# One order of summing and turning the values' product, a new hand-written order of attention, more zero matmuls in the bias stage

## The chip, the core and the metric

The kernel runs on one core of a Trainium2 chip. The metric is device time in microseconds (us). Before the change three runs took 933.37 to 933.82 us, median 933.52 us.

## What is computed

Four batches of 576 positions go through attention with 8 heads of 64, then an MLP with layer norm (512 to 2048 to 512), then a gated MLP that mixes positions. Everything is float32. The part around the change, cut:

```python
scores = scale * q @ k.T                       # per batch and head, 576 x 576
x = log1p(|i - j|) / log1p(max(i, 1))
scores += relu(x[..., None] * w1 + b1) @ w2    # one bias matrix per head
attn = exp(scores - max); attn /= attn.sum(-1) + 1e-9
out = attn @ v                                 # back to rows of 512
x = out + relu(layernorm(out) @ w_ch1) @ w_ch2
...
```

## The kernel before, in words

Products that need float32 accuracy are done in pieces: a value is split into a part rounded to the fast matmul type (hi) and a rest (lo), and hi x hi, lo x hi and hi x lo are added in PSUM.

**Stages.** (1) The bias stage builds the bias of all heads: VectorE (line 335) and ScalarE (line 333) make relu pieces, TensorE sums them over the hidden units (line 347), VectorE or ScalarE scales them (lines 354, 356), and DMAs write them to DRAM and read them back in the layout of the scores. Matmuls of zeros (`busy`, line 293) are put in at the start (`WARM` = 8) and ahead of the sums of the steps in `FILL` (9 of the 36 steps, one each). (2) Attention runs over 16 units: a unit is a pair of heads (hp) of one batch (b), in the order hp outer, b inner. (3) The first MLP, (4) the gated MLP.

**One attention unit** has nine score tiles n = 0 to 8 of 128 query rows (tile 4 holds the last 64 rows of both heads). For a tile, S is the scores' matmul (line 705, four of 288 columns, eight for n = 4), add is the bias add with the row minimum on VectorE (line 711), exp is ScalarE's exponential with the row sum (line 725), T turns the 128x512 weights in four transposes (line 731), hi is ScalarE's rounded copy out of PSUM and lo is VectorE's rest (lines 118, 121). The last 64 keys go another way: RT turns them (lines 739, 741), RThi and RTlo split them, and RTd (lines 769, 771) is a DMA that moves the rest to the other half of the partitions; RTx splits straight into place instead of RTlo and RTd. PV multiplies with the values (line 813), nine matmuls for each head h and half x of the columns; the rt one is the ninth.

**The end of a unit before the change.** The values are stored as hi and lo side by side, so PV gives 128 rows: 64 of the main part and 64 of the lo part, still turned (head dimension on partitions). Pev (line 816, ScalarE) copies 128x288 to `Psb`. O (line 819) turns a 128x128 block of one head, four per head, eight per unit. Oev (line 824, ScalarE) copies the four blocks to `Ob`. fo (line 830, GpSimd) adds the two parts, once per head. fx (line 842, GpSimd) multiplies by the reciprocal row sum, once per head, and a DMA stores 512 rows to DRAM (line 845). The last 64 rows go by oc, Or (line 853), xr (lines 862, 863) and stores at line 867. ra and rb make the reciprocals.

**What sets the order.** Each engine takes its instructions in the order in which the program emits them, and so does the SP queue, from which nearly all DMAs are issued: a DMA that waits holds up those behind it. Lists of words give that order: `FIRST` for unit 0, `SEQ` for every later unit ("0 T 3" is this unit's tile 3, "-1" the unit before, "1" the unit after), `END` for the tail of unit 15 with the first MLP tiles (H). `slot n` marks a place where side work is issued: at slot 0 `place_q` (line 237) puts the next unit's queries in place with four DMAs, at slot 1 the stores of line 867, at slot 5 the loads of a later unit's q and k. kh and vh split the next unit's keys and values on GpSimd, sq splits queries. C and cp are steps of converting the MLP's weights (line 161 to 178, five VectorE steps per piece, two steps in each of units 2 to 11). The rows of attention's output of batch 0 are read back for the MLP (four DMAs, line 626) at slot 8 of unit 13, those of batch 1 at slot 8 of unit 15, and layer norm is spread behind them.

The score tiles alternate between two PSUM buffers (`SB`) and the transposes between two (`PA`), so S of a tile waits for the add two tiles earlier, and T for the lo two tiles earlier.

Of the kernel before, what the change touches and what calls it, by code (L numbers as in the profile page):

```python
# [43 lines left out]
    PV 0 1 8 9, hi 8, slot 7, +S 4, lo 7, +exp 1, slot 8, Pev 0 1
# [57 lines left out]
def block_kernel(  # L102
# [484 lines left out]
    def open_first():  # L587
# [32 lines left out]
        for b in range(2):  # L620
            x = M["x", b] = []

            def loads(b=b, x=x):
                for t in range(4):
                    x.append(M["stage"].tile([128, DM], F32, name="t"))
                    sp.dma_start(out=x[t], in_=xs[b][128 * t:128 * t + 128])

            M["loads", 12 + 2 * b] = loads
        for q, j in enumerate(LN_AT):
            for (b, t) in j:  # L630
                v, j = 13 + (q + 1) // 2, (q + 1) % 2
                if v == 14:
                    conv_at.setdefault((v, 2), []).append(lambda b=b, t=t: ln_stats(b, M["x", b][t], M["x", b][t], act if b else pool))
                    continue
                then = conv_at.setdefault((v, j + 1), []).append
                conv_at.setdefault((v, j), []).append(lambda b=b, t=t, f=then: ln_stats(b, M["x", b][t], M["x", b][t], act if b else pool, f))
        for t, p in enumerate(AP_AT):
            when(*p, lambda t=t: ln_apply(0, t))
# [825 lines left out]
```

## Time and profile before

| | |
|---|---|
| median of three runs | 933.52 us |
| profiled execution, its own time | 936.71 us |
| its span from first to last instruction | 934.9 us |
| TensorE matmul busy | 914.6 us, 98% of the span |
| VectorE / ScalarE / GpSimd busy | 716.4 / 494.7 / 419.0 us |
| chain that ended last | TensorE 86%, VectorE 6%, DMA 3% |

The profile is of one execution, which has a time of its own. Busy shares are averages over stages with different limits, so they are read by stage. A matmul's duration holds the time in the pipeline; what a matmul adds to a run of them is the distance from one start to the next.

### The profile page before, as it was taken

Reading aid. Unit: us, or ns where it says so; the run is one execution under the profiler, and the core shown is the slowest. Engines: PE = TensorE matmul, PEld = TensorE weight load, DVE = VectorE, ACT = ScalarE, POOL = GpSimd, SP = SyncE. Lnnn points to the kernel's source line nnn. Section 1 sums busy time; section 2 is a strip of 40 time slices with the busy share of each in tenths; the row PEclk is TensorE's granted clock in tenths of the full one; section 3 lists DMA queues with packets and bytes.
Section 4 is the critical chain, followed back from the end, with each engine's and each line's share of the span. In section 5 each row is a group of like instructions: output and inputs, shape, how many; then the busy total and the mean of one; then the engine's idle time right before and its main releaser. Section 6 shows DMA issues by size and latency. Waiting matters only on the chain.

```text
span 934.9 us, 15977 instructions
## 1 busy us (share of the span) xinstructions
PE 914.6 (98%) x5617; PEld 798.7 (85%) x5617; DVE 716.4 (77%) x1390; ACT 494.7 (53%) x1092; POOL 419.0 (45%) x547
## 2 busy tenths in 40 slices
PE   7899999999999999999999999999999999999998
PEld 2279999999998888888888888888888998989996
DVE  7999999999888777877689897989665656455452
ACT  8989999999997653222131322222132635253340
POOL 0058888888897543322233343333200534243241
PEclk9999999999999999999999999999999999999999
DMA  6888767767762641121212323342313000001001
GB/s 222 283 265 276 238 189 243 218 210 216 231 197 63 214 163 46 56 89 34 89 56 89 126 87 123 101 123 89 102 68 127 1 1 34 12 1 57 1 35 67
DMA packets 64623, 113.18 MB, mean 121 GB/s; under 512 B 13216, under 2 KB 27680, under 8 KB 64288
## 3 DMA queue, kind: packets, MB, share of 16 engines
q1 hardware_dynamic: 64240, 111.74, 37.9%
q8 instruction: 44, 0.72, 0.3%
q10 hardware_dynamic: 304, 0.43, 0.1%
q14 instruction: 35, 0.29, 0.1%
HBM read 70.33 MB, written 28.38 MB: 106 GB/s over the span
## 4 chain that ended last, share of the span: by engine, by line
PE 86%; DVE 6%; DMA 3%; POOL 2%; ACT 2%; issue 1%; SPq 0%; POOLq 0%; DVEq 0%; ACTq 0%
PE psh L125 21%; PE psy L125 21%; PE psa L125 11%; PE s L705 6%; PE psa L1308 6%; PE PB L813 6%; PE psa L1290 5%; PE pt L731 5%; DVE m L335 4%; PE pt L486 1%; PE OB L819 1%; DMA q<-q 1%; DMA rt<-tl 1%; PE s L741 1%; PE pt L347 1%
## 5 line engine op out<-in xcount | busy, mean ns | idle before, releaser
L125 PE MATMUL psh<-blk,w1h 128*128 128x512 f32 (+1 forms) x640 | 151.2, 368 | 0.0
L654 ACT ACTIVATE hh<-psh 128x512 fp32r<-128x512 f32 (+1 forms) x80 | 44.1, 554 | 198.6 <-PE psh L125 198.5
L177 POOL TENSOR_TENSOR cvl<-cvl,cvt 128x512 f32<-128x512 f32 x44 | 56.9, 1293 | 205.4 <-DVE cvt L174 185.9
L125 PEld LDWEIGHTS psh<-blk,w1h 128*128 128x128 f32 x640 | 113.4, 189 | 20.5
L725 ACT ACTIVATE a<-ct,sm 128x576 f32<-128x576 f32 x144 | 112.1, 781 | 2.6 <-DVE sm L711 2.6
L711 DVE CUSTOM_DVE_ANT_0 ct<-s,bias 128x576 f32<-128x576 f32 x144 | 106.3, 747 | 5.4 <-PE s L705 3.5
L1111 DVE TENSOR_TENSOR x_sb<-psy,x_sb 128x512 f32<-128x512 f32 x144 | 97.3, 683 | 9.5 <-PE psy L125 9.0
L655 DVE SCALAR_TENSOR_TENSOR hl<-psh,hh 128x512 fp32r<-128x512 f32 (+1 forms) x80 | 50.5, 633 | 57.2 <-ACT hh L654 57.2
L125 PE MATMUL psy<-w2h,hh 128*128 128x512 f32 x288 | 90.1, 394 | 0.0
L125 PE MATMUL psy<-w2l,hh 128*128 128x512 f32 x288 | 88.9, 390 | 0.0
L125 PE MATMUL psy<-w2h,hl 128*128 128x512 f32 x288 | 88.8, 389 | 0.0
L731 PE MATMUL pt<-ident,a 128*128 128x128 f32 x576 | 84.4, 274 | 0.4 <-DVE at0l L121 0.4
L125 PE MATMUL psh<-blk,w1l 128*128 128x512 f32 (+1 forms) x320 | 79.0, 368 | 0.0
L705 PE MATMUL s<-kh,q 128*128 128x288 f32 x320 | 75.3, 325 | 3.2 <-DMA q<-q 2.1
L731 PEld LDWEIGHTS pt<-ident,a 128*128 128x128 f32 x576 | 68.6, 142 | 1.1 <-DVE at0l L121 0.7
L705 PE MATMUL s<-kl,q 128*128 128x288 f32 x320 | 65.7, 295 | 0.0
L125 PEld LDWEIGHTS psh<-blk,w1l 128*128 128x128 f32 x320 | 56.8, 189 | 10.0
L125 PEld LDWEIGHTS psy<-w2h,hl 128*128 128x128 f32 x288 | 54.1, 188 | 11.5
L125 PEld LDWEIGHTS psy<-w2l,hh 128*128 128x128 f32 x288 | 54.0, 188 | 11.5
L178 POOL TENSOR_TENSOR cvw<-cvl,cvw 128x512 f32<-128x512 f32 x44 | 59.9, 1362 | 3.4
L125 PEld LDWEIGHTS psy<-w2h,hh 128*128 128x128 f32 x288 | 52.6, 188 | 9.6
L121 DVE TENSOR_TENSOR at1l<-pt,at1h 128x512 fp32r<-128x512 f32 (+1 forms) x80 | 50.3, 630 | 9.3 <-ACT at1h L118 9.2
(185 smaller groups left out, 2126.7 us busy)
## 6 DMA issues: line engine op xcount, KB each, us to landing
r<-in_moe_w_ch_dram SPq DMA_DIRECT2D x32, 512.0 KB, 4.6
k<-in_k_dram SPq DMA_DIRECT2D x16, 640.0 KB, 4.4
q<-q SPq DMA_DIRECT2D x64, 144.0 KB, 3.4
scr<-o SPq DMA_DIRECT2D x24, 295.5 KB, 3.4
v<-in_v_dram SPq DMA_DIRECT2D x16, 320.0 KB, 5.1
q<-in_q_dram SPq DMA_DIRECT2D x16, 288.0 KB, 3.1
wc<-cvw SPq DMA_DIRECT2D x16, 256.0 KB, 2.5
x_sb<-xs SPq DMA_DIRECT2D x4, 1024.0 KB, 7.1
```

What stands on the lines that cost most here:

```text
L121: (eng or dve).tensor_tensor(out=o, in0=i, in1=hi.bitcast(F32), op=ALU.subtract)
L125: pe.matmul(ps, lhsT=w, rhs=x, start=start and j == 0, stop=stop and j == len(terms) - 1)
L177: pool.tensor_tensor(out=T["l"], in0=T["l"], in1=T["t"].bitcast(F32), op=ALU.mult)
L178: pool.tensor_tensor(out=T["w"], in0=T["l"], in1=T["w"], op=ALU.add)
L655: dve.scalar_tensor_tensor(out=hl[:, f, :n], in0=ps[:, :n], scalar=0.0, in1=hh[:, f, :n].bitcast(F32), op0=ALU.max, op1=ALU.subtract)
L705: pe.matmul(s[:, x, :288], lhsT=w, rhs=m[:, 288 * x:288 * x + 288], start=j == 0, stop=j == len(prs) - 1)
L711: dve.tensor_tensor_reduce(out=ct, in0=s[:, :, :288], in1=bias[UNITS[u][0]][:, n].rearrange("p (a b) -> p a b", a=2), scale=-0.125, scalar ...
L725: act.activation(weights(n), ct.rearrange("p a b -> p (a b)"), AF.Exp, scale=-1.0, bias=mt, accum_out=SU[u % 2][:, n:n + 1])
L731: pe.transpose(PA[k % 2][:, j], e[:, 128 * j:128 * j + 128], ident)
L813: pe.matmul(d, lhsT=w, rhs=m, start=q == 0, stop=q == len(terms) - 1)
L1111: dve.tensor_tensor(out=x_sb[:, t], in0=ps, in1=x_sb[:, t], op=ALU.add)
L1308: pe.matmul(ps[:, z, :288], lhsT=v, rhs=w[:, 288 * z:288 * z + 288], start=(q == 0), stop=(q == len(terms) - 1))
```

## The change

Units 1 to 14 no longer turn both parts of both heads. `Pd` moves the half of the 128 rows that has to change partitions by a DMA (64x512, one per head), `Ps` adds it to the other half on GpSimd (64x512, one per head), and the two heads' sums lie on top of each other in `whole`. Four transposes `Q` turn it, and fx multiplies by the reciprocals straight out of PSUM on VectorE. Unit 0 and unit 15 keep O, Oev and fo. `SEQ` and `END` are new, `FIRST` covers units 0 and 1 and `END` units 14 and 15 (SEQ now runs for u = 2 to 13). The reads of batch 0 and batch 1 (LD) and the layer norm steps (LN, LS, LP, FT, F) are words of `END`. `WARM` is 12, and `FILL` gives 21 zero matmuls over 14 steps. Bias loads of hp 0 are placed at other words.

```diff
-FILL = (0, 4, 8, 12, 16, 20, 24, 28, 32)
+FILL = {0: 1, 4: 1, 6: 1, 8: 6, 10: 1, 11: 1, 12: 1, 14: 3, 15: 1, 16: 1, 20: 1, 24: 1, 28: 1, 32: 1}
-WARM = 8
+WARM = 12
-            if y in FILL:
-                busy(1)
+            busy(FILL.get(y, 0))
...
+        moved, whole = (Ob[:, z].rearrange("p a b -> p (a b)") for z in range(2))
+        def emit_Pd(u, h):
+            sp.dma_start(out=moved[half(1 - h)].rearrange("p (x c) -> p x c", x=2), in_=ends(Psb[half(h), h]))
+        def emit_Ps(u, h):
+            o, i, j = (t[half(1 - h)] for t in (whole, Psb[:, h], moved))
+            pool.tensor_tensor(out=o.rearrange("p (x c) -> p x c", x=2), in0=ends(i), in1=j.rearrange("p (x c) -> p x c", x=2), op=ALU.add)
+        def ends(p):
+            return bass.AP(p.tensor, p.offset, [list(p.ap[0]), [320, 2], [1, 256]])
+        def emit_Q(u, t):
+            o = (0, 256, 128, 384)[t]
+            pe.transpose(OB[:, 128 * t:128 * t + 128], whole[:, o:o + 128], ident)
...
         def emit_fx(u):
...
+            if u not in xt:
+                x = xp.tile([128, 4, 2, D], F32, name="x")
+                z = 18 + 9 * (u % 2)
+                f = sm[:, z:z + 10].rearrange("p (h a) -> p a h", h=2)[:, :4].unsqueeze(3).to_broadcast([128, 4, 2, D])
+                dve.tensor_tensor(out=x, in0=OB.rearrange("p (a h d) -> p a h d", a=4, h=2), in1=f, op=ALU.mult)
```

The new `SEQ`, whole:

```python
0 slot 0, -1 lo 8, 0 B 0, 0 add 3, 0 exp 2, 0 T 0, 0 exp 3, -1 PV 1 0 0 5, -1 PV 1 0 5 8, -1 PV 1 0 8 9, 0 hi 0, 0 slot 1, 0 add 4, -1 Pev 1 0,
0 RT 1 0, 0 S 5, 0 exp 4, 0 RT 3 0, -1 Pd 0, 0 RThi 0, 0 C 0, 0 S 6, 0 T 1, -1 PV 1 1 0 1, 0 lo 0, 0 T 2, 0 C 1, 0 hi 1, 0 add 6, -1 PV 1 1 1 8,
0 add 5, -1 PV 1 1 8 9, 0 lo 1, 0 hi 2, 0 S 7, 0 slot 2, 0 lo 2, 0 RT 4 0, 0 exp 5, -1 Pev 1 1, 0 slot 3, 0 T 3, 0 T 4, 0 RThi 2, 0 RTlo 0, 0 kh,
-1 Pd 1, 0 S 8, 0 hi 3, 0 hi 4, 0 add 7, 0 exp 6, 1 S 0, 0 RTd 0, 0 lo 3, 0 PV 0 0 0 2, 0 T 5, 0 slot 4, 0 RTlo 2, 0 lo 4, 0 exp 7, 0 RTd 2,
0 slot 5, 0 add 8, 0 PV 0 0 2 8, 0 T 6, 0 vh, -1 oc, 1 S 1, 0 hi 5, 1 add 0, 0 exp 8, 1 S 2, 0 lo 5, 0 RT 8 1, 1 add 1, 0 RT 6 1, -1 Ps 0,
0 PV 0 0 8 9, 0 hi 6, -1 Or, -1 Ps 1, 0 lo 6, 0 T 7, 0 RThi 1, -1 ra, -1 Q 3, 0 Pev 0 0, -1 Q 0, -1 rb, 0 RTlo 1, -1 Q 1, 0 RTd 1, -1 Q 2, 0 T 8,
0 B 1, 1 add 2, 0 PV 0 1 0 8, 0 cp, 0 PV 0 1 8 9, 1 S 3, 1 S 4, -1 fx, 1 exp 0, 0 hi 7, 0 sq, 0 hi 8, 0 slot 6, 0 lo 7, 0 slot 7, -1 xr, 1 exp 1,
0 Pev 0 1, 0 slot 8
```

The part of the new `END` that the prediction speaks of (unit 14, from its start to the turns of unit 13):

```python
14 slot 0, 14 add 3, 14 exp 2, 14 exp 3, 14 LD 0 0, 14 S 5, 14 T 0, 14 hi 0, 13 lo 8, 14 LD 0 1, 14 slot 1,
...
14 S 8, 13 Ps 0, 14 RT 4 0, 13 Pev 1 0, 14 lo 2, 13 PV 1 1 0 1, 14 RTlo 0, 14 exp 6, 14 LD 0 3, 14 hi 3, 13 PV 1 1 1 8, 13 PV 1 1 8 9, 14 T 4,
14 add 8, 14 slot 5, 13 Pev 1 1, 14 RThi 2, 14 lo 3, 14 LN 1, 14 hi 4, 15 S 0, 15 S 1, 14 PV 0 0 0 2, 14 exp 7, 14 RT 6 1, 14 exp 8, 14 lo 4, 14 T 5,
14 vh, 14 RTlo 2, 14 T 6, 14 RTd 0, 14 PV 0 0 2 8, 15 add 0, 15 S 2, 13 oc, 15 add 1, 14 hi 5, 13 Pd 1, 14 lo 5, 13 Ps 1, 13 Q 2, 13 Q 1, 14 RTd 2,
...
```

## Rows read from the trace of the kernel before

**Rows 1.** The page, part 1: busy time, share of the span, instructions.

```profile
PE 914.6 (98%) x5617; PEld 798.7 (85%) x5617; DVE 716.4 (77%) x1390; ACT 494.7 (53%) x1092; POOL 419.0 (45%) x547
```

**Rows 2.** Stretches: length, busy PE, PEld, DVE, ACT, POOL (instructions), clock, DMA share, GB/s.

```profile
0.00:52.39 52.39, 40.91 (x370) 12.92 (x370) 47.01 (x132) 45.58 (x101) 2.12 (x11) 1.00 0.75 254
52.39:71.02 18.63, 17.57 (x128) 15.58 (x124) 16.91 (x41) 15.81 (x41) 11.57 (x11) 1.00 0.84 270
86.55:102.87 16.32, 15.88 (x128) 15.41 (x127) 15.31 (x36) 15.46 (x41) 13.75 (x19) 1.00 0.74 221
149.47:165.00 15.53, 15.53 (x128) 15.53 (x127) 14.41 (x36) 15.02 (x40) 14.05 (x15) 1.00 0.80 251
273.71:293.92 20.21, 18.07 (x134) 17.76 (x132) 15.76 (x39) 15.95 (x43) 14.28 (x25) 0.92 0.44 112
```

**Rows 3.** TensorE by time: start, us, operation, count, idle time before with its releaser.

```profile
130.28 1.04 PE L731 MATMUL pt<-ident,a 128*128 128x128 f32 x8
...
131.69 0.69 PE L813 MATMUL PB<-at0l,v 128*64 128x288 f32 x4
132.22 0.29 PE L813 MATMUL PB<-rt,v 128*128 128x288 f32 x1
...
284.62 0.51 PE L705 MATMUL s<-kh,q 128*128 128x288 f32 x2 [2.14 <-DMA q<-q]
```

**Rows 4.** One stretch of 1 us behind that wait; columns as in rows 2.

```profile
286.00:287.00 1.00, 1.00 (x6) 1.00 (x6) 0.97 (x4) 0.13 (x1) 0.00 (x0) 0.50 0.00 0
```

**Rows 5.** SP queue by time, ahead of that wait: start, us, DMA, count.

```profile
270.70 0.38 SPq L845 DMA_DIRECT2D xs<-x  x1
...
275.58 1.76 SPq L626 DMA_DIRECT2D t<-xs  x4
277.43 2.40 SPq L237 DMA_DIRECT2D q<-q  x4
```

**Rows 6.** Groups removed, or nearest to what is added: busy us, mean ns, idle before.

```profile
L819 PE MATMUL OB<-ident,psb 128*128 128x128 f32 x128 | 24.5, 272 | 0.0
L830 POOL TENSOR_TENSOR x<-ob 128x256 f32<-128x256 f32 x30 | 22.1, 736 | 8.6 <-ACT ob L824 5.7 <-PE pt L731 2.9
L842 POOL TENSOR_TENSOR x<-x,sm 128x256 f32<-128x256 f32 x30 | 17.9, 618 | 0.0
L121 POOL TENSOR_TENSOR vre<-v,vre 64x512 fp32r<-64x512 f32 x2 | 2.6, 1291 | 0.2
L1340 DVE TENSOR_TENSOR v<-psa,x_sb 128x512 f32<-128x512 f32 x18 | 12.4, 688 | 21.2 <-PE psa L125 13.7 <-POOL blk L121 7.5
```

**Rows 7.** VectorE by time, two neighbouring instructions inside unit 4.

```profile
125.78 0.69 DVE L121 TENSOR_TENSOR at0l<-pt,at0h 128x512 fp32r<-128x512 f32 x1
126.38 0.75 DVE L711 CUSTOM_DVE_ANT_0 ct<-s,bias 128x576 f32<-128x576 f32 x1
```

**Rows 8.** Line 771: its issue on the SP queue and its landing.

```profile
L771 SPq DMA_DIRECT2D rt<-tl x14: 634/638/657, 94.1 to 301.0; - x14
DMA to landing us min/median/max: 1.9/2.5/3.7
```

**Rows 9.** GpSimd by time in unit 14: the keys' first step, the values' last.

```profile
275.37 0.73 POOL L115 TENSOR_SCALAR kh<-k 128x640 fp32r<-128x640 f32 x1
...
282.23 1.54 POOL L121 TENSOR_TENSOR v<-v,v 128x640 fp32r<-128x640 f32 x1
```

**Rows 10.** TensorE by time in the bias stage: zeros, and the sums behind two holes.

```profile
1.03 4.21 PE L293 MATMUL pt<-zero 128*128 128x512 f32 x9 [1.03 <-DVE zero L288]
6.64 2.33 PE L347 MATMUL pt<-m,W 128*32 128x320 f32 x24 [1.41 <-DVE m L335]
...
16.25 1.68 PE L347 MATMUL pt<-m,W 128*32 128x448 f32 x16 [1.63 <-DVE m L335]
```

**Rows 11.** TensorE's waits between 73 and 310 us.

```profile
PE pt L731 <- DVE at0l L121: 0.4, 1, 0.4
PE PB L813 <- DMA rt<-tl: 0.3, 1, 0.3
```

More of the change, by code (lines that the diff above doesn't have):

```diff
@@ L44 @@
[L44 removed]
+    0 S 0, 0 add 0, 0 slot 0, 0 slot 1, 0 S 1, 0 S 2, 0 add 1, 0 exp 0, 0 T 0, 0 S 5, 0 exp 1, 0 add 2, 0 RT 1 0, 0 hi 0, 0 T 1, 0 exp 2, 0 add 5, 0 C 0,
+    0 S 3, 0 S 6, 0 lo 0, 0 C 1, 0 add 3, 0 slot 2, 0 add 6, 0 T 2, 0 exp 5, 0 slot 3, 0 S 4, 0 hi 1, 0 hi 2, 0 S 7, 0 exp 3, 0 lo 2, 0 RT 3 0, 0 exp 6,
+    0 T 3, 0 lo 1, 0 add 4, 0 RThi 0, 0 RTx 0, 0 hi 3, 0 T 5, 0 S 8, 0 kh, 0 exp 4, 0 RT 6 1, 0 hi 5, 0 slot 4, 0 RT 4 0, 0 lo 3, 0 add 7, 0 T 4, 1 S 0,
@@ L45 @@
+    2 add 1, 1 Pev 0 0, 0 Oev 1, 2 S 2, 0 fo 1, 1 RTx 1, 2 exp 0, 0 fx, 1 T 7, 0 Or, 1 sq, 2 add 2, 1 B 0, 1 T 8, 1 slot 6, 1 hi 7, 1 PV 0 1 0 8,
+    1 PV 0 1 8 9, 1 hi 8, 2 exp 1, 1 slot 7, 1 lo 7, 0 xr, 1 Pev 0 1, 1 slot 8, 2 S 3, 2 S 4
 """.split(",")]
-B_AT = [(0,), (1, 2), (3,), (4, 5), (6,), (7, 8)]
-LN_AT = [(), (), ((0, 0), (0, 1)), ((0, 2), (0, 3)), ()]
-AP_AT = [(15, 0), (15, 1), (15, 4), (15, 5)]
+B_AT = [[(), (0,), (1, 2), (3, 4), (5, 6), (7, 8)], [(0,), (1, 2), (3,), (4, 5), (6,), (7, 8)]]
@@ new lines @@
+    14 LS 0, 14 PV 0 0 8 9, 14 hi 6, 14 lo 6, 13 Or, 14 LS 1, 13 Q 3, 13 Q 0, 15 LN 2, 15 exp 0, 13 fx, 15 exp 1, 14 T 8, 14 slot 6, 14 slot 7,
+    14 RT 8 1, 14 T 7, 15 S 3, 14 ra, 14 Pev 0 0, 13 xr, 14 RThi 1, 14 hi 7, 14 slot 8, 14 hi 8, 15 add 2, 15 slot 0, 15 RT 1 0, 15 LN 3, 15 LS 2,
+    14 PV 0 1 0 8, 15 LS 3, 14 PV 0 1 8 9, 15 slot 1, 15 LP 0, 15 add 3, 14 lo 7, 15 S 4, 14 RTlo 1, 15 exp 2, 14 lo 8, 15 slot 2, 15 add 4, 15 S 5,
+    15 LP 1, 14 Pev 0 1, 14 RTd 1, 15 exp 3, 15 T 0, 15 RT 3 0, 14 PV 1 0 0 5, 15 hi 0, 15 RThi 0, 15 slot 3, 14 PV 1 0 5 8, 15 lo 0, 15 add 5, 15 T 1,
@@ new lines @@
+    15 exp 4, 15 hi 1, 15 S 6, 14 PV 1 0 8 9, 15 RTlo 0, 15 T 2, 15 lo 1, 14 Pev 1 0, 15 RT 4 0, 15 exp 5, 15 S 7, 15 slot 4, 14 PV 1 1 0 1,
+    14 PV 1 1 1 8, 15 add 6, 14 PV 1 1 8 9, 15 S 8, 15 hi 2, 15 RTd 0, 14 Pd 0, 15 exp 6, 15 add 7, 15 slot 5, 15 T 3, 14 Pev 1 1, 15 RThi 2, 15 lo 2,
+    15 LP 2, 15 RTlo 2, 14 Pd 1, 14 Ps 0, 16 FT 0, 15 add 8, 15 hi 3, 15 lo 3, 16 F 0, 15 T 4, 15 RTd 2, 15 hi 4, 15 lo 4, 16 FT 1, 15 T 5, 14 Ps 1,
+    15 PV 0 0 0 2, 16 FT 2, 15 PV 0 0 2 8, 14 rb, 15 PV 0 0 8 9, 14 oc, 14 Q 2, 14 Q 3, 15 exp 7, 16 F 1, 16 F 2, 15 hi 5, 15 Pev 0 0, 15 exp 8, 14 Q 0,
@@ L525, in ln_two @@
     def ln_two(j):
-        x = M["x", 1][2 * j:2 * j + 2]
+        x = [M["x", 1][2 * j + q] for q in range(2)]
         mv, rs = (M["two"][:, 8 * j + 4 * q:8 * j + 4 * q + 4].rearrange("p (a b) -> p a b", a=2) for q in range(2))
@@ L619, in open_first @@
         xT[0] = block_pair(M["wa0"])
[L620 to L638, printed above, removed]
+        M["x", 0], M["x", 1] = {}, {}
+        xn[0] = {}
     def h_tile(ch, blk, f, a=0, b=12):
@@ L919, in emit_slot, with emit_LD, emit_LN @@
                 open_first()
-            if n == 8 and ("loads", u - 1) in M:
-                M["loads", u - 1]()
         emit = dict(
             slot=emit_slot, B=emit_B, sq=emit_sq, kh=emit_kh, vh=emit_vh, C=emit_C, cp=lambda u: emit_C(u, 2), S=emit_S, add=emit_add, exp=emit_exp, T=emit_T, hi=emit_hi, lo=emit_lo, RT=emit_RT, RThi=emit_RThi,
-            RTlo=emit_RTlo, RTd=emit_RTd, RTx=emit_RTx, PV=emit_PV, Pev=emit_Pev, O=emit_O, Oev=emit_Oev, fo=emit_fo, fx=emit_fx, Or=emit_Or, oc=emit_oc, ra=emit_ra, rb=emit_rb, xr=emit_xr,
+            RTlo=emit_RTlo, RTd=emit_RTd, RTx=emit_RTx, PV=emit_PV, Pd=emit_Pd, Ps=emit_Ps, Q=emit_Q, Pev=emit_Pev, O=emit_O, Oev=emit_Oev, fo=emit_fo, fx=emit_fx, Or=emit_Or, oc=emit_oc, ra=emit_ra, rb=emit_rb, xr=emit_xr,
         )
+        def emit_LD(u, b, t):
+            x = M["x", b][t] = M["stage"].tile([128, DM], F32, name="t")
+            sp.dma_start(out=x, in_=xs[b][128 * t:128 * t + 128])
+        def emit_LN(u, t):
+            x = M["x", 0][t]
+            stats, scale, apply = norm_parts(M["sm"], x, 1e-6, x, pool)
+            stats()
+            xn[0][t] = x, apply, scale
         def first_T(j):
```

77 lines of the change are left out of this document (38 added, 39 removed).

## The prediction

> **What bounds the kernel now.** I read the page first: TensorE is busy for 914.6 of 934.9 us [rows 1]. A busy share says nothing about single stages, so the busy time by stretch comes next [rows 2]. In the bias stage (0 to 52.39 us) VectorE is busy for 47.01 and ScalarE for 45.58 us, TensorE for 40.91: those two set the pace there. In attention it turns round. A middle unit lasts 15.53 us and TensorE is busy for all of it; ScalarE has 15.02, VectorE 14.41, GpSimd 14.05 us. Two stretches stand out: unit 2 with 16.32 us and unit 14 with 20.21 us. The MLPs come after 312 us and the change leaves their matmuls alone. So the edit pays in attention by what it takes off TensorE, if no other engine takes over, and by the stalls that the new order avoids or adds.
>
> **Fewer transposes.** A transpose's mean duration is 272 ns [rows 6], but that holds the way through the pipeline. Eight in a row took 1.04 us [rows 3], so each further one costs (1.04 - 0.27) / 7 = 0.11 us. Four matmuls of 288 columns take 132.22 - 131.69 = 0.53 us to the next start, 0.13 each [rows 3]. The list of a unit (76 matmuls, 50 transposes) then sums to 15.47 us, against 15.53 measured [rows 2], so these prices may be used. Units 1 to 14 turn four blocks in place of eight: 14 x 4 = 56 transposes fewer, 56 x 0.11 = **-6.2 us**, and a unit of about 15.05 to 15.1 us. The Trainium skill (TensorE: Matmul & The Clock Gate, Part 4: PE-mode transpose) gives about 275 ns for one in a kernel's context; as a duration the trace agrees (272 ns), as a cost eight in 1.04 us speak against it; by it the term would be -15.4 us.
>
> **The other engines.** ScalarE loses two 128x512 copies per unit, which nobody waited for long. GpSimd loses two fo (736 ns) and two fx (618 ns), 2.71 us, and gains two Ps; an add of that very shape, 64x512, took 1291 ns [rows 6], so 2.58 us: even. VectorE gains fx. Its nearest row is a 128x512 add that reads PSUM, 688 ns [rows 6]; from start to start such an operation takes 126.38 - 125.78 = 0.60 us [rows 7]. Then VectorE has 14.41 + 0.60 = 15.0 us in a unit of 15.1. ScalarE runs today at 15.02 of 15.53 without TensorE waiting for it, so this need not fail, but there is no room: I take 0.1 us in each of the ten units with conversion steps, **+1.0 us** (bounds: 0, if the order hides it; 4, if each loses 0.4).
>
> **The stall before unit 15.** TensorE waited 2.14 us for the queries of unit 15 [rows 3]. On the SP queue the store of unit 12 went out at 270.70, the four reads of the same rows had to wait for it and went at 275.58, and the queries stood behind them until 277.43 [rows 5]. In the new order slot 0 of unit 14, which issues these queries, stands ahead of LD 0 0, so this wait goes: **-2.1 us**. What is late next is the subject of the next but one part. Behind the wait the granted clock was 0.50, so 1.2 GHz [rows 4]; over the 20.21 us of unit 14 it was 0.92 [rows 2], that is 0.08 x 20.21 / 0.5 = 3.2 us at half speed, which cost 1.6 us: **-1.6 us** if no wait like it comes in its place. The rest of unit 14's excess I leave where it is.
>
> **Unit 2** is 16.32 - 15.53 = 0.8 us too long, with a wait of 0.4 us for a lo [rows 2, 11]. It lies in the old SEQ's first turns, which the new FIRST replaces: **-0.8 us** (bound 0). The opening, 18.63 us with 17.57 busy [rows 2], is replaced too; I see nothing that decides it: 0, between -1 and +1.
>
> **A new wait in unit 14.** Now TensorE needs GpSimd inside the unit: Pev, Pd, Ps, then Q. LD 0 0 still waits for unit 12's store, which now goes out some 13 us into unit 13; 275.58 - 270.70 = 4.9 us later [rows 5] is 2.8 us into unit 14. Behind it on the SP queue stand LD 0 1 (1.76 / 4 = 0.44 us to issue), two stores of slot 1 and Pd 0, each about 0.64 us, and a DMA of this kind lands 2.5 us after its issue [rows 5, 8]: Pd 0 lands at 2.8 + 0.9 + 1.2 + 2.5 = 7.4 us. On GpSimd the run from kh to the end of v took 283.77 - 275.37 = 8.4 us from 1.66 us into unit 14 [rows 9], with one fo and a small wait in it. With two Ps in place of that fo and Ps 0 held until 7.4, Ps 1 ends at about 12.4 us. TensorE's list reaches Q 2 at 10.6 us. I take a wait of 1.8: **+1.8 us**. Bounds: 0 (GpSimd starts earlier) and 3.4 (the clock falls again for 1.6).
>
> **RTd 2.** In the new SEQ RTlo 2 comes after lo 3 on VectorE, by the summed steps at 8.2 us of a unit; its DMA lands 2.5 us later, at most 3.7 [rows 8], so at 10.7; TensorE's ninth matmul of PV 0 0, which reads it, stands at 10.7. Today such a wait occurs once in the attention, 0.3 us [rows 11]. I take 0.1 us for each of the 12 turns of SEQ, **+1.2 us** (bounds 0 and 6, with 0.5 each). RTd 1 has more room than now: the store that waits for fx stands behind it instead of ahead.
>
> **Zeros.** Nine zero matmuls took 4.21 us at the start, at most 0.47 each, and the first sums then waited 1.41 us for VectorE [rows 10]. Four more end at most 0.5 us late, five more at step 8, where 1.63 us were idle, 0.7 us late. VectorE and ScalarE set this stage, and the clock is at 1.00 all through it [rows 2]: I take 0, between 0 and +1.2; their cover is the idle time of TensorE.
>
> **Sum.** -6.2 + 1.0 - 2.1 - 1.6 - 0.8 + 1.8 + 1.2 = -6.7 us. The profiled execution took 936.71 us, which would become 930.0. The median of the runs is 3.2 us lower than that execution; the same difference on 933.52 gives **926.8 us**. 0.2% is 1.9 us, about what can be told from no change: faster means below 931.7, slower above 935.4.
>
> **Rivals.** (1) *GpSimd sets attention, slower.* In a unit kh, Ps 0, v, oc and Ps 1 take some 9.9 us and stand ahead of Q on GpSimd. TensorE reaches Q 3 at 11.4 us, so kh must start by 1.5 us. It started 1.66 us into unit 14 [rows 9]; it can start from 0.5 us, when xr of the unit before is through, because sq has to wait for less. Each microsecond beyond 1.5 costs 12 us over SEQ. The forecast turns into slower from (1.9 + 6.7) / 12 = 0.7 us per unit, that is kh at 2.2 us or two Ps of 1.65 us; at 1.0 us per unit it gives 933.5 - 6.7 + 12 = 939 us. For it: GpSimd's 14.05 of 15.53 us; against: in most units no cp is due. The Trainium skill (GPSIMD Engine Reference, 1. Specifications) says that GpSimd shares its SBUF interfaces with VectorE; no row here shows a Ps-like add above 1.29 us on average. Chance 0.10. (2) *VectorE becomes the bound, no change.* It loses 0.4 us in each of the 12 units (4.8), RTd 2 costs 0.3 (3.6, in place of 2.2 for both) and unit 14's wait brings the half clock back (+1.6): 926.8 + 6.2 + 1.6 = 934.6 at worst, 931.7 to 934.6 with part of it. For it: 15.0 of 15.1 us; against: ScalarE at 97% today costs nothing. Chance 0.11. (3) *The new waits don't come.* Then -6.2 - 2.1 - 1.6 - 0.8 = -10.7, with the opening's bound -11.7: 922 to 923. Chance 0.22. (4) *Each transpose is worth its duration:* 56 x 0.272 = 15.2 in place of 6.2, 917.8 us. Eight in 1.04 us exclude it nearly. Chance 0.02. The forecast itself, 924 to 931.7, has 0.55.
>
> **How the numbers follow.** Faster is the forecast with (3) and (4), 0.79; the same 0.11; slower 0.10. The range holds the forecast and (3), and of (2) the nearer part, so 921.5 to 933.
>
> **What would show it.** Right: 16 + 56 = 72 transposes into OB; middle units of 15.05 to 15.2 us with TensorE busy throughout; no wait of S for the queries before unit 15; a wait of Q for Ps in unit 14 of 1 to 3 us and none in the units before. Wrong: Q waiting for GpSimd in every unit (1); units of 15.4 us with T or S waiting for lo or add (2); PV's rt matmul waiting for its DMA in most units; a stretch at half clock in unit 14; a bias stage longer than 52.4 us.

## The result, and the profile after

The kernel after took 940.89 us (median of 6 runs, 939.99 to 942.47), the kernel before beside it 933.58 us (933.02 to 933.82): ratio 1.0079, 95% interval 1.0066 to 1.0092. It is **slower by 7.3 us**, where 6.7 us less were forecast, and lies outside the range. From the first MLP on nothing changed: its first transposes stand at 318.69 us in the profile before and at 322.41 us in the one after, 3.7 us later, and the spans, 934.9 and 938.8 us, differ by 3.9. The bias stage is nearly as long as before (52.39 and 52.51 us). So the question lies in attention.

Page, part 1, of the kernel after (answers to [rows 1]):

```profile
PE 915.7 (98%) x5577; PEld 794.5 (85%) x5577; DVE 726.1 (77%) x1404; ACT 486.4 (52%) x1064; POOL 419.3 (45%) x519
```

TensorE's busy share is 98% as before, and would tell nothing. Busy time by stretch, kernel after, columns as in [rows 2]: the bias stage, then three middle units.

```profile
0.00:52.51 52.51, 45.62 (x386) 16.52 (x386) 46.98 (x132) 45.59 (x101) 2.24 (x11) 1.00 0.75 252
132.69:148.39 15.70, 15.65 (x124) 15.09 (x123) 15.70 (x39) 14.44 (x37) 15.08 (x15) 1.00 0.78 217
197.68:212.86 15.18, 15.18 (x124) 15.06 (x124) 14.51 (x37) 14.08 (x37) 13.31 (x16) 1.00 0.68 186
148.39:165.04 16.65, 15.38 (x124) 15.12 (x123) 15.82 (x39) 15.07 (x39) 12.26 (x13) 1.00 0.86 255
```

The reader sees three kinds of unit. In the third row TensorE works throughout and the unit is 15.18 us, as forecast; three units are like this (15.15, 15.18, 15.11). In the second, VectorE is busy for all of 15.70 us. In the fourth, TensorE is busy for 15.38 of 16.65 us; it waits for the rest. What for is in its waits from 73 to 310 us (answers to [rows 11]):

```profile
PE PB L819 <- DMA rt<-tl: 6.6, 8, 2.7
PE OB L838 <- POOL ob L831: 2.4, 3, 1.0
PE s L711 <- DVE sm L717: 0.9, 1, 0.9
```

The ninth matmul of PV waits for the rest of the last keys eight times. Before, it did so once, for 0.3 us.

The groups that the change removes and adds, kernel after (answers to [rows 6]):

```profile
L838 PE MATMUL OB<-ident,ob 128*128 128x128 f32 x56 | 8.8, 277 | 2.4 <-POOL ob L831 2.4
L841 PE MATMUL OB<-ident,psb 128*128 128x128 f32 x16 | 3.9, 272 | 0.0
L867 DVE TENSOR_TENSOR x<-OB,sm 128x512 f32<-128x512 f32 x14 | 9.6, 686 | 1.3 <-PE OB L838 1.3
```

72 transposes into OB in place of 128, and fx on VectorE at 686 ns, as its nearest row gave.

**One late unit, followed.** Kernel after, the SP queue, then TensorE, VectorE and GpSimd by time, around the wait of 1.27 us at the end of the unit 148.39 to 165.04:

```profile
157.13 1.10 SPq L896 DMA_DIRECT2D xs<-xr  x2
158.34 0.63 SPq L827 DMA_DIRECT2D ob<-psb  x1
159.01 0.59 SPq L589 DMA_DIRECT2D r<-in_moe_w_ch_dram  x1
159.70 0.62 SPq L827 DMA_DIRECT2D ob<-psb  x1
160.42 1.19 SPq L775 DMA_DIRECT2D rt<-tl  x2
161.70 0.62 SPq L777 DMA_DIRECT2D rt<-tl  x1
```

```profile
158.39 0.41 DVE L145 TENSOR_TENSOR tl<-s,rt 128x256 fp32r<-128x256 f32 x1
...
160.05 0.27 DVE L145 TENSOR_TENSOR tl<-s,rt 64x128 fp32r<-64x128 f32 x1
```

```profile
164.83 0.37 PE L819 MATMUL PB<-rt,v 128*128 128x288 f32 x1 [1.27 <-DMA rt<-tl]
```

```profile
164.30 1.27 POOL L831 TENSOR_TENSOR ob<-psb,ob 64x512 f32<-64x512 f32 x1 [2.21 <-DMA ob<-psb]
165.66 0.20 POOL L855 TENSOR_SCALAR sm<-sm 128x9 f32<-128x9 f32 x1
```

```profile
165.89 0.22 DVE L858 RECIPROCAL sm<-sm 128x9 f32<-128x9 f32 x1 [1.68 <-POOL sm L855]
166.07 0.42 DVE L145 TENSOR_TENSOR tl<-s,rt 128x256 fp32r<-128x256 f32 x1
```

RTlo 0 is done at 158.80 us and RTlo 2 at 160.32, but SP issues one DMA behind the other and comes to RTd 0 only at 160.42 and to RTd 2 at 161.70. Pd 1, issued at 159.70 right behind a load of 512 KB, lands 4.6 us later, so Ps 1 starts at 164.30. Behind Ps 1 on GpSimd stands ra, and VectorE's rb waits 1.68 us for it; behind rb stand RTlo 1 and RTd 1. So one late transfer is handed on: SP, Pd, Ps, ra, rb, RTlo 1. VectorE waited for ra 6 times, 7.7 us, in the kernel after; before, this wait is not among VectorE's.

That SP itself is late shows at RTd 2 (line 771 before, 777 after; ns, least/median/most, of the queue's wait for RTlo 2):

```profile
L771 SPq EVENT_SEMAPHORE  x14: 28/1174/6319, 91.9 to 294.6; - x14
```

```profile
L777 SPq EVENT_SEMAPHORE  x14: 17/17/17, 96.2 to 305.2; - x14
...
who waited for it (us, times):
  PE PB L819: 5.6, 5
  PEld PB L819: 0.6, 1
```

Before, RTd 2 went out ahead of RTd 0; SP was there first and waited 1.2 us (median) for VectorE. After, both Pd and the two issues of RTd 0 stand ahead of RTd 2, and its data always waited for SP, up to 2.1 us. That alone need not cost anything: at RTd 0 SP never waited in the kernel before either, and TensorE lost 0.3 us there.

**What ended the eight waits.** Late landings ended most of them. In three units (at 110.36, 159.01 and 191.63 us) a load of 512 KB of the MLP's weights is issued between Pd 0 and Pd 1. The first of them on the SP queue, TensorE's wait behind it, and that period (columns as in [rows 2]):

```profile
110.36 0.61 SPq L587 DMA_DIRECT2D r<-in_moe_w_ch_dram  x1
111.06 0.62 SPq L827 DMA_DIRECT2D ob<-psb  x1
111.78 1.19 SPq L775 DMA_DIRECT2D rt<-tl  x2
113.06 0.99 SPq L777 DMA_DIRECT2D rt<-tl  x1
```

```profile
117.33 0.37 PE L819 MATMUL PB<-rt,v 128*128 128x288 f32 x1 [2.70 <-DMA rt<-tl]
```

```profile
99.25:117.54 18.29, 15.59 (x124) 15.12 (x123) 16.04 (x39) 15.06 (x39) 12.47 (x13) 1.00 0.90 267
```

Over all units, line 777 (RTd 2) lands so long after its issue:

```profile
DMA to landing us min/median/max: 1.9/1.9/4.1
```

In the three units Pd 1, RTd 0 and RTd 2 landed 3.0 to 5.4 us after their issue, each behind the load; in the other units between 120 and 250 us the two Pd, RTd 0 and RTd 2 took 1.9 to 2.5 us. The waits in the three units are 2.70, 1.27 and 0.39 us, 4.4 of the 6.6. Had RTd 2 landed in 1.9 us there too, some 0.6 us would be left of them (an estimate from the times of its issues). Three more waits (0.21, 0.19 and 0.68 us) are for RTd 1, which landed 4.8 to 5.3 us after its issue, shortly behind the loads of k and v. In the last two (0.92 and 0.28 us) RTd 2 landed in 2.0 us, so only SP's lateness is left. In the kernel before the same weight loads are there, but RTd 2 and RTd 0 landed in 2.0 to 3.7 us, and no wait came of it.

### The profile page after: what moved, and what is told of

It reads as the page before. It is cut to its first block, busy times and chain, and to the rows that moved or that the text cites. A ratio compares the mean times of both kernels' runs of the same rounds, so it can differ in the third digit from the quotient of the medians.

```text
span 938.8 us, 15923 instructions
## 1 busy us (share of the span) xinstructions
PE 915.7 (98%) x5577; PEld 794.5 (85%) x5577; DVE 726.1 (77%) x1404; ACT 486.4 (52%) x1064; POOL 419.3 (45%) x519
## 4 chain that ended last, share of the span: by engine, by line
PE 79%; POOL 8%; DMA 5%; DVE 4%; issue 2%; ACT 1%; SPq 0%; POOLq 0%; DVEq 0%
PE psh L149 21%; PE psy L149 21%; PE psa L149 10%; PE psa L1341 6%; PE psa L1323 5%; PE s L711 4%; PE PB L819 3%; PE pt L737 3%; DMA rt<-tl 3%; DVE m L359 2%; POOL kl L145 2%; PE pt L509 1%; POOL ob L831 1%; POOL v L145 1%; PE pt L371 1%
## 5 line engine op out<-in xcount | busy, mean ns | idle before, releaser
L711 PE MATMUL s<-kh,q 128*128 128x288 f32 x320 | 72.7, 317 | 1.8 <-DVE sm L717 1.5
L711 PEld LDWEIGHTS s<-kh,q 128*128 128x128 f32 x320 | 48.7, 189 | 5.1 <-DVE sm L717 3.0
```

The source lines that it names most:

```text
L711: pe.matmul(s[:, x, :288], lhsT=w, rhs=m[:, 288 * x:288 * x + 288], start=j == 0, stop=j == len(prs) - 1)
```

## The experiments

Ratios are to the kernel before, run beside each kernel on the same chip; its medians there were 933.6 to 935.9 us, so ratios are compared, not times. The interval behind each is 95%. The waits are those of one profiled execution of each kernel.

| kernel | us | ratio | TensorE waits for rt / Q, 73 to 340 us |
|---|---|---|---|
| after | 940.89 | 1.0079 | 6.6 / 2.4 |
| q_first | 933.11 | 0.999 | none / none |
| old_order_q | 957.73 | 1.0262 | 2.2 / 9.5 |
| old_zeros | 941.03 | 1.0068 | 7.6 / 1.1 |
| rtx2 | 939.97 | 1.0054 | 4.8 / 1.3 |
| sp_more | 942.47 | 1.0094 | 9.5 / 2.8 |
| one_store | 940.46 | 1.0069 | 5.8 / 1.9 |
| sp_late | 953.91 | 1.0198 | 17.3 / 1.7 |
| kv_late, rtx2_kv_late | 963.66, 966.13 | 1.0323, 1.0348 | not read; 7.5 / 7.6 |
| pd_act | 942.0 | 1.008 | 3.4 / 3.1 |
| ra_early | 938.85 | 1.0053 | 3.8 / 3.4 |
| ra_early_rtx2 | 938.01 | 1.0041 | 3.6 / 2.9 |
| ra_early_rtx_all | 946.13 | 1.0130 | none / 1.4 |
| no_conv | 940.25 | 1.0055 | 6.3 / 2.8 |
| q_first_no_conv | 935.16 | 0.9994 | 1.0 / none |
| c_moved, ra_rtx2_c_moved | 955.51, 956.20 | 1.0217, 1.0229 | 1.4 / 2.7; 1.2 / 1.8 |
| all_mended | 938.91 | 1.0046 | 2.0 / 1.6 |

**Was the wait before unit 15 there to be won? (q_first)** The kernel before, with the queries of unit 15 issued ahead of the reads of batch 0.

```diff
-            if n == 8 and ("loads", u - 1) in M:
-                M["loads", u - 1]()
+            if (n == 1 and u == 14) or (n == 8 and u == 15):
+                M["loads", 12 if u == 14 else 14]()
```

> The kernel before, with the four reads of batch 0's rows issued at slot 1 of unit 14, behind the queries of unit 15, instead of at slot 8 of unit 13. If the 2.1 us wait of the profiled execution is there in every run, this gains 2 us (and up to 1.6 more where the clock fell behind it): 930 to 931.5. If it was a matter of that one execution: 933.5.

0.999 (0.998 to 1.000). Its trace has neither the wait of 2.14 us nor the half clock: unit 14 is a unit like the others. Busy time of the unit that held the wait:

```profile
271.33:286.86 15.53, 15.53 (x128) 15.53 (x127) 13.94 (x37) 15.02 (x40) 12.99 (x18) 1.00 0.65 190
```

So taking wait and slow clock away, 3.7 us by the forecast's prices, brought 1.9 us at most in timed runs: they belonged to the one profiled execution, which was 3.2 us above its median. q_first's profile is therefore the better one to lay beside the kernel after. Fifteen periods, from one Or (line 853 before, 882 after) to the next, the last a short one, from 83.3 us (83.65 in the kernel after) to the end of attention, summed, first q_first, then the kernel after (PE, PEld, DVE, ACT, POOL):

```profile
sum 228.20, PE 226.67 PEld 223.54 DVE 208.09 ACT 217.61 POOL 196.43; mean PE 15.11 PEld 14.90 DVE 13.87 ACT 14.51 POOL 13.10
```

```profile
sum 234.44, PE 223.85 PEld 217.07 DVE 217.40 ACT 208.88 POOL 198.03; mean PE 14.92 PEld 14.47 DVE 14.49 ACT 13.93 POOL 13.20
```

Attention is 6.2 us longer: TensorE is busy for 2.8 us less and idle for 10.6 in place of 1.5 us, 9.1 more. Its weight loads fell by 6.5 us, near the 6.2 of the forecast. Of the 10.6 us, rt has 6.6, Q 2.4 and S 0.9. A wait costs more than TensorE's idle time shows: in the six periods with rt waits TensorE is busy for 15.34 to 15.59 us, in the three without a stall for 15.11 to 15.18 us, with the same weight loads (15.0 to 15.1 us). The eleven periods from 99.25 to 275.64 us take 9.7 us more than eleven of 15.15 us would; 8.7 of them lie in the six with rt waits, 1.0 in two (15.70 and 15.61 us) in which VectorE is busy throughout.

**Summing first alone (old_order_q).** q_first with Pd, Ps, Q and the new fx put into the old SEQ for units 1 to 14.

```diff
-    0 slot 1, -1 PV 1 0 0 5, ... 0 RTd 0, ... -1 fo 0, ... 0 vh, 0 cp, ... 0 T 8,
+    0 slot 1, -1 Pd 0, -1 PV 1 0 0 5, ... 0 RTd 0, -1 Pd 1, ... -1 fo 0, -1 Ps 0, ... 0 vh, -1 Ps 1, 0 cp, ... 0 T 8, -1 Q 3, -1 Q 0, -1 Q 1, -1 Q 2,
```

> The kernel before with one part of the change alone: the sum first and four transposes for units 1 to 14, put into the old order (Pd 0 at slot 1, Pd 1 behind RTd 0, Ps where fo stood, Q behind T 8), and the reads of batch 0 behind the queries as in q_first. Theory A (the transposes are worth 6.2 us, the new order loses them in its queue): 5 to 7 us under q_first, about 925 to 927. Theory B (summing first costs VectorE and GpSimd what TensorE saves): equal to q_first or slower. In the old order RTd 0 and RTd 2 keep their place ahead of PV.

1.0262 (1.0234 to 1.0290). Waits of TensorE and of GpSimd, 83 to 312 us:

```profile
PE OB L832 <- POOL ob L825: 9.5, 9, 2.1
```

```profile
POOL ob L825 <- DMA ob<-psb: 23.0, 13, 4.0
```

It is slower, as theory B said, but by the wait for the transfers, not by VectorE's or GpSimd's work. The cheaper sum costs far more than its 6.2 us when its chain (Pev, transfer, add, turn) is put into an order that leaves it no time. How far a better placing in the old order would go was not tried, nor was the new order with the old ending (O, Oev, fo), so what the order by itself costs or brings stays open.

**The zeros (old_zeros).** The kernel after with the old `WARM` and `FILL`.

> The changed kernel with the old zeros (8 at the start, 9 single ones). Zeros have no part (theories A and B alike): within 1 us of the changed kernel's 940.9, bias stage 52.4 us either way, clock 1.00 in it. If the zeros' price is real (rival C), it is faster by 0.5 to 1.2 us.

1.0068 (1.0052 to 1.0084), as the kernel after. The first S starts at 52.08 us in it and at 52.51 us in the kernel after; in the kernel before and in q_first, whose bias stages are the same, at 52.39 and 52.90 us. So the zeros cost and bring nothing that shows. Its attention is that of the kernel after, and the rt waits are 7.6 in place of 6.6 us: by so much they differ from one execution to another.

**Fewer and more issues on SP (rtx2, sp_more, one_store).** rtx2 splits RT 2 straight into place; sp_more cuts the first transfer of RTd 0 into two halves of its columns; one_store issues the two stores of the last 64 rows as one.

```diff
-0 RTlo 2, 0 lo 4, 0 exp 7, 0 RTd 2,
+0 RTx 2, 0 lo 4, 0 exp 7,
```

```diff
-                for h in range(2):
-                    sp.dma_start(out=xs[b][512:, 128 * hp + D * h:128 * hp + D * h + D], in_=xr[64 * h:64 * h + 64])
+                o = xs[b][512:, 128 * hp:128 * hp + 128].rearrange("r (h c) -> h r c", h=2)
+                sp.dma_start(out=o, in_=xr)
```

> The changed kernel, but in SEQ the small rest of the last keys (RTlo 2, RTd 2) is written straight into place by VectorE (RTx 2), without its DMA. Theory A, the SP queue reaches RTd 0 and RTd 2 too late: the last DMA ahead of the waiting rt matmul is gone, TensorE's waits for rt fall from 6.6 us to under 2.5, the time from 940.9 to about 936. Theory B, VectorE at its limit sets the units and the rt wait only shows it: the wait turns up at another place and the time stays at 940 to 942. No work is left out.

> The kernel after with one more issue on the SP queue in each unit and no byte more: the first transfer of RTd 0 is cut into two of half its columns, some 0.6 us of SP's time in units 2 to 15. Theory A (SP's issue time, 12 of 15 us per unit, decides when RTd and Pd go out): rt waits and waits of Ps for Pd grow, 944 to 950 us. If the transfers are late only because they land behind the large loads: 940 to 942 us, rt waits 6 to 7.5 us as before.

> The kernel after with the two stores of the last 64 rows of a unit (two heads, 64 partitions each) issued as one transfer of the same bytes: one issue of some 0.55 us fewer on the SP queue per unit, ahead of Pd 0, and nothing else. Theory A (SP's issues decide when RTd and Pd go out): rt waits 3 to 5 us in place of 6.6, 937 to 939.5 us, the mirror of the run with one issue more (942.5). If the landing alone decides: 940 to 941.5 us and rt waits of 6 to 7 us.

rtx2 1.0054 (1.0036 to 1.0072), sp_more 1.0094 (1.0080 to 1.0108), one_store 1.0069 (1.0049 to 1.0089). With one issue more the rt waits are 9.5 us, with one fewer 5.8, which is no further from 6.6 than old_zeros is; the intervals of the times overlap with that of the kernel after. Theory A's 944 to 950 and 937 to 939.5 us were both missed; where the landing alone decides, 940 to 942 and 940 to 941.5 us had been expected, and 942.5 and 940.5 came. One issue is not what decides. In rtx2, where RTd 2 is gone from SEQ, TensorE still waits 4.8 us for the transfers that are left, 2.7 of them in the three units with a weight load; the time is theory B's 940. The waits behind the first two weight loads, at about 116 and 164 us, are also in the traces of old_zeros, sp_more, one_store, pd_act, ra_early, ra_early_rtx2, no_conv and all_mended. No run moved these loads alone.

**Other orders on SP (sp_late, kv_late, rtx2_kv_late) and another queue (pd_act).** sp_late issues the stores of slot 1 at slot 5 and B 0 behind vh; kv_late issues the loads of k and v behind RTd 1; pd_act issues Pd from ScalarE.

```diff
-            sp.dma_start(out=moved[half(1 - h)]
+            act.dma_start(out=moved[half(1 - h)]
```

> The changed kernel, but in SEQ the two stores of the last 64 rows go from slot 1 to slot 5 and the bias loads B 0 behind vh, so that 1.1 us and, in the units that load bias, another 0.5 to 1.3 us of issues stand behind RTd 2 on the SP queue instead of ahead of Pd 0. Theory A: RTd 0 and RTd 2 go out 1 to 2 us sooner, TensorE's waits for rt fall from 6.6 us to about 1, the time to about 935. Theory B: same waits under another name, 940 to 942.

> The changed kernel, but in SEQ the loads of k and v (960 KB together) are issued right behind RTd 1 instead of just ahead of it. Theory A2, the small moves of rt land late because large loads were issued shortly before them: RTd 1 lands in about 2.5 us instead of up to 5.3, the waits of the first rt matmul of a unit go (about 2.5 us in the trace of the changed kernel), the time falls from 940.9 to about 938; the waits at RTd 0 and RTd 2 stay. Theory A1, only the place in the SP queue counts: no gain, since k and v now stand ahead of the next unit's queue: 941 to 945.

> Both edits together: no DMA for the last keys' small rest, and k and v behind RTd 1. Theory A (A1 and A2 together): the two kinds of rt wait go, TensorE's waits for rt fall under 2 us, the time to 934 to 937. Theory B (VectorE or GpSimd would set the units anyway): 940.

> The changed kernel with the moves Pd issued from ScalarE's queue instead of SP's. Theory A: 1.2 us of issues less ahead of RTd 0 on SP, rt waits fall to some 2.5 us, the time to about 937, unless ScalarE, which must wait out two issues per unit, gives it back. Theory B: 940 or more.

sp_late 1.0198 (1.0176 to 1.0220), 953.9 us: the opposite of relief, and beyond both theories. With the stores gone from slot 1, a Pd comes to the head of the queue before ScalarE is ready for it, and holds everything behind it. The SP queue's waits at Pd, and TensorE's:

```profile
SPq L827 <- ACT rt L142: 32.3, 15, 4.3
```

```profile
PE PB L819 <- DMA rt<-tl: 17.3, 12, 3.1
```

The rt waits now fall on RTd 1 (17.0 of the 17.3 us; 2.80 us at 247.64 us): what had been moved back stood ahead of it, and there it landed 4.1 to 7.4 us after its issue. RTd 0 and RTd 2, held up together with Pd, went out 2.4 to 5.4 us behind the three weight loads in place of 1.4 to 2.7, landed in 1.9 to 2.9 us, and no wait is left at them in these units. That is as near as the runs come to a test of the landings. kv_late 1.0323 (1.0306 to 1.0341) and rtx2_kv_late 1.0348 (1.0327 to 1.0368) missed all their forecasts: the keys come late, and GpSimd's kh with them (16.0 us of waits for k, read in rtx2_kv_late alone), and Ps and Q behind it. This is rival 1, provoked. pd_act 1.008 (1.006 to 1.010): two issues fewer on SP go with rt waits of 3.4 us, half of those of the kernel after, but VectorE then waits 8.3 us for ScalarE's hi in place of 2.5 (of `at0h`), and nothing is won. The Trainium skill (DMA: Bandwidth & Descriptors, Issuing engines are not separate DMA queues) says that issuing from more engines saves only the sequencer's time. The trace agrees: SP's time was saved, and behind the weight loads RTd 2 still landed 3.3 to 4.6 us after its issue.

**The hand-on through ra (ra_early, ra_early_rtx2).** ra is issued ahead of vh, so VectorE's rb no longer waits for Ps 1; then with RTx 2 as well.

```diff
-... 0 T 6, 0 vh, ... -1 Ps 1, 0 lo 6, 0 T 7, 0 RThi 1, -1 ra, -1 Q 3,
+... 0 T 6, -1 ra, 0 vh, ... -1 Ps 1, 0 lo 6, 0 T 7, 0 RThi 1, -1 Q 3,
```

> The kernel after, with the first step of the reciprocals (ra, GpSimd) issued ahead of the values' split instead of behind Ps 1, in all turns of SEQ. In the kernel after, VectorE waited 7.7 us in 6 waits (2.9 at most) for that step, which stood on GpSimd behind Ps 1, which waited for Pd; behind VectorE's wait stand RTlo 1 and so RTd 1. Theory C (this chain, Pd late, Ps late, ra late, VectorE held, RTd 1 late, is how one late transfer is handed on from unit to unit): VectorE's wait for ra is 0, waits for rt at TensorE fall from 6.6 to 3 us or less, 935 to 938 us in place of 940.9. Theory A (the issues on the SP queue alone): VectorE's wait for ra goes, but the rt waits stay at 5 to 7 us, 939.5 to 941.5 us.

> The same with RTx 2 in place of RTlo 2 and RTd 2, one transfer fewer on SP per unit. Theory C: 934 to 937 us, rt waits under 2 us. Theory A: 938.5 to 940.5 us, as with RTx 2 alone (940.0).

ra_early 1.0053 (1.0040 to 1.0067): VectorE's 7.7 us of waits for ra are gone, as both theories said. The rt waits are 3.8 us in place of 6.6, between theory C's 3 and theory A's 5, in a profiled execution that was the fastest of its five; the time of 938.9 us lies between the two forecasts too. VectorE's waits for Q (fx) rose from 1.3 to 4.3 us. With RTx 2 1.0041 (1.0028 to 1.0055), 938.0 us, between theory C's 937 and theory A's 938.5, with rt waits of 3.6 us where theory C said under 2. The link is shown (the wait is gone, and the time falls by 2.6 thousandths, with intervals that just touch), but it is not the whole.

**Is it VectorE? (ra_early_rtx_all, no_conv, q_first_no_conv, c_moved, ra_rtx2_c_moved)**

```diff
-0 RTlo 0, ... 0 RTd 0, ... 0 RTlo 2, ... 0 RTd 2, ... 0 RTlo 1, ... 0 RTd 1,
+0 RTx 0, ... 0 RTx 2, ... 0 RTx 1,
```

```diff
+        if skip:
+            t1 = t2 = t3 = t4 = lambda: None
```

```diff
-0 RThi 0, 0 C 0, 0 S 6, ... 0 T 2, 0 C 1, ... 0 lo 2,
+0 RThi 0, 0 S 6, ... 0 T 2, ... 0 lo 2, 0 C 0, 0 C 1,
```

> ra early, and RTx 0, 1 and 2 in place of all RTlo and RTd in the turns of SEQ: no transfer of the last keys' rest is left in units 2 to 13, VectorE has two more instructions per unit, about 0.6 us more. If the rt transfers hold all that was lost: waits for rt 0, units of 15.2 to 15.4 us, 929 to 932 us. If VectorE is full, as its 15.00 of 15.00 us say: units of 15.6 to 15.8 us that end in waits of S or T for VectorE, 936 to 940 us. If the chain of Pd, Ps and Q takes over: waits of Q for Ps of 3 us and more in units 2 to 13, about 938 us.

> The kernel after without the VectorE steps that convert the first MLP's weights (5 for each of 4 pieces, 18.9 us in all; ScalarE writes a scaled copy in their place, so the weights' values are left out). Theory V (VectorE is the bound in the units with long conversion steps, and late rests, transfers and reciprocals follow from it): VectorE 13.5 to 14.3 us per unit, rt waits under 3 us, 930 to 935 us. Theory A (SP's issues and landings alone): rt waits 5 to 7 us, 938.5 to 941 us.

> The control: the kernel before, with the reads of batch 0 behind the queries as in q_first, without the same VectorE steps. Both theories: TensorE sets the unit at 15.53 us, so the time stays within 1.5 us of 933.1 us; a fall of 2 us or more would say that the steps cost in the old order too.

> The kernel after with both conversion steps of a unit of SEQ behind lo 2, where GpSimd mostly waits for the last product of the unit before (ahead of the values' split), instead of ahead of and behind lo 0, where kh and kl run. If a step that starts while GpSimd works on kl or kh is held until that ends: the 20 steps fall from 18.9 us towards the 11 us that they take alone, below 15 us at any rate, and the time to 936 to 939 us. If they are held there too, or if RTlo 0, now behind them, is what is late: 940 to 944 us.

> The three together: ra early, RTx 2, conversion steps behind lo 2. Theory V: 933 to 936.5 us, the fastest of these, at best as fast as the kernel before. Theory A: 937 to 939 us, as with the first two alone (938.0).

Without any transfer of the last keys' rest (1.0130, 1.0116 to 1.0144) the time, 946.1 us, is beyond all three forecasts. In the units with conversion steps VectorE is busy nearly throughout; in those without it is not (14.95 of 16.18 us). One of each:

```profile
150.10:166.75 16.65, 15.97 (x125) 15.17 (x123) 16.45 (x39) 14.44 (x37) 12.86 (x13) 1.00 0.76 227
249.94:266.12 16.18, 15.63 (x124) 15.16 (x123) 14.95 (x37) 14.31 (x37) 14.70 (x17) 1.00 0.74 231
```

But without the conversion's VectorE steps the kernel after comes to 1.0055 (1.0037 to 1.0072) only, no more than each other link gave: 940.3 us and 6.3 us of rt waits, as theory A said, where theory V said 930 to 935 us. VectorE is at 13.1 to 14.4 us per unit, and TensorE waits as before:

```profile
PE PB L825 <- DMA rt<-tl: 6.3, 9, 1.5
```

So theory V fell: VectorE's full hands are not what makes the transfers late. The control, q_first_no_conv (0.9994, 0.9978 to 1.0009), is level with the kernel before. Neither run prices the steps exactly: ScalarE's copy in their place costs something too (in the control TensorE waits 1.0 us for exp, which q_first does not show, and four periods of the units with these steps take 16.0 us in place of 15.5 to 15.8).

c_moved (1.0217, 1.0200 to 1.0235) and ra_rtx2_c_moved (1.0229, 1.0213 to 1.0244) were to put the conversion where GpSimd waits. It went wrong, beyond both forecasts of each run, and shows why the steps are long at all. VectorE and GpSimd by time:

```profile
143.45 0.82 DVE L189 SCALAR_TENSOR_TENSOR cvw<-r,cvt 128x512 int32<-128x512 int32 x1
144.31 1.66 DVE L192 TENSOR_SCALAR cvt<-r 128x512 int32<-128x512 int32 x1
```

```profile
143.01 0.73 POOL L139 TENSOR_SCALAR v<-v 128x640 fp32r<-128x640 f32 x1 [1.02 <-PE PB L819]
143.82 1.86 POOL L145 TENSOR_TENSOR v<-v,v 128x640 fp32r<-128x640 f32 x1
145.65 0.47 POOL L139 TENSOR_SCALAR pr<-psb 128x128 f32<-128x128 f32 x1
```

The step of line 192 starts 0.5 us into GpSimd's v and ends 0.3 us behind it; in q_first the same step took 0.42 to 0.70 us. In c_moved the 20 steps sum to 23.9 us, in the kernel after to 18.9, in q_first to 14.4. RTlo 0 and the adds stand behind them on VectorE, and S waited 18.3 us in nine units (the profile names GpSimd's oc, which ends 0.95 us before S starts in this one).

**Everything together (all_mended).** ra early, RTx 2, the one store, and the four Q behind T 8.

```diff
-... 0 RThi 1, -1 Q 3, 0 Pev 0 0, -1 Q 0, -1 rb, 0 RTlo 1, -1 Q 1, 0 RTd 1, -1 Q 2, 0 T 8,
+... 0 RThi 1, 0 Pev 0 0, -1 rb, 0 RTlo 1, 0 RTd 1, 0 T 8, -1 Q 3, -1 Q 0, -1 Q 1, -1 Q 2,
```

> ra early, RTx 2, the one store, and the four Q (with fx) behind T 8 instead of around Pev and RTlo 1, so that Ps has 0.5 us more. If the handed-on lateness of SP's queue, Pd, Ps and RTd is the whole loss in the turns of SEQ: rt and Q waits of SEQ together under 3 us, units of 15.1 to 15.5 us, 931 to 935 us, level with the kernel before or a little faster. If something else holds these units: 936.5 to 938.5 us, as with ra early and RTx 2 alone (938.0).

1.0046 (1.0030 to 1.0063), 938.9 us (937.9 beside a kernel before of 933.58): not the 931 to 935 us of the first case, but the second, something else holds these units. In the turns of SEQ no Q waits any longer (the 1.6 us are in the last units), and rt waits are 2.0 us. Yet units with conversion steps take 16 us; two of them, and one without such steps:

```profile
148.11:164.34 16.23, 15.72 (x125) 15.09 (x124) 15.91 (x39) 15.14 (x39) 11.90 (x13) 1.00 0.83 247
211.28:227.31 16.03, 15.85 (x124) 15.11 (x123) 15.79 (x37) 14.66 (x37) 14.82 (x15) 1.00 0.82 246
259.31:274.64 15.33, 15.33 (x123) 15.08 (x123) 13.28 (x33) 14.09 (x35) 14.27 (x18) 1.00 0.79 241
```

VectorE is busy for 15.8 to 15.9 us of these two, the 20 conversion steps take 19.2 us, and TensorE now waits ten times for a lo of VectorE's (1.8 us in all; once, 0.2 us, in the kernel after). This speaks for VectorE taking the transfers' place; it is not shown, since all_mended without the conversion's steps was not run, and one period of 16.37 us has VectorE at 14.71 us. None of the 18 kernels beat the kernel before; q_first and its control are level with it.

## Why the prediction was wrong

- **The transposes, right.** 56 fewer at 0.11 us. Weight loads fell by 6.5 us over attention, and units without a stall take 15.11 to 15.18 us, where 15.05 to 15.2 was said. Rival 4 (272 ns each) is out.
- **The stall before unit 15 and the half clock (-2.1 and -1.6), counted twice.** The profiled execution was 3.2 us above the median. I subtracted these stalls from its time and then moved the sum to the median by the same 3.2 us again. q_first shows that the median held at most 1.9 us of these 3.7, and probably next to nothing. Without this step the sum would have been 930.5 us.
- **RTd 2, +1.2 us: the failed step.** I let its DMA go out when RTlo 2 was done and land 2.5 us later, at most 3.7. In the kernel after SP comes to it up to 2.1 us behind the data, and in the three units with a weight load ahead of it the transfer took 3.0 to 4.1 us. TensorE waits 5.6 us for RTd 0 and RTd 2, in five units, where 1.2 were allotted; most of it lies in those three units. I had walked VectorE's and TensorE's lists, but not SP's, where both Pd, the load and RTd 0 stand ahead of RTd 2. "RTd 1 has more room than now" failed with it: TensorE waits 1.1 us for RTd 1, for which I had put nothing, and rb, RTlo 1 and RTd 1 now wait for Ps 1 through ra, a wait that the list of words shows and that I had not followed. Together the rt waits are 6.6 us and, with what they cost beyond idle time, some 8.7, by the count of periods above. That is 7.5 more than allotted, of the 10.4 us between 930.5 and the measured 940.9.
- **VectorE, +1.0 us.** fx was priced rightly (686 ns). The conversion steps at their new words meet GpSimd's kl and take 18.9 us in place of 14.4, which I had not seen; in the kernel after the two periods that VectorE fills lose 1.0 us by it. Leaving the steps out gives 2.4 thousandths between the ratios and leaves the transfers late (no_conv).
- **The wait of Q in unit 14, +1.8 us: the sum near, the place not.** There are three waits, in units 13, 14 and 15, of 0.82, 0.58 and 1.00 us, 2.4 in sum, without a slow clock; only 0.58 lies in the unit that was forecast.
- **Unit 2, -0.8 us.** The first period fell from 16.33 us (kernel before) to 15.60, as forecast, but one of 18.29 us follows, with the longest rt wait, 2.70 us.
- **Zeros, 0:** nothing shows against it. **Rival 1**, the one slower case, had GpSimd as the late engine, with Q waiting in every unit; in the turns of SEQ Q waited once, in the last. Its chain (Pd, Ps) is late at times, but there it reached TensorE by way of ra, VectorE and RTd 1.

What is shown: the rt waits, and the hand-on through ra (2.6 thousandths between the two ratios). What the traces of ten kernels bear out, but no run tested by itself: that the weight loads ahead of RTd 0 and RTd 2 make them land late. What is argued only: that Pd's issues are what makes SP late; no run took Pd away from all queues. So the cause of the whole loss stays open in part. No single link holds it: each one mended gives 0 to 3 thousandths, with intervals that mostly overlap, and in all_mended VectorE, at 15 to 16 us of such units, may be late instead.
